# Low halves of eight weight tiles on GpSimd, one pair pooled by products with ones, and a new plan of the order

## The chip, the cores and the metric

The kernel runs on one core of a Trainium2 chip. Its engines are TensorE (PE: matmuls, with PEld for weight loads), VectorE (DVE), ScalarE (ACT), GpSimd (POOL) and SyncE (SP, which issues most DMAs). Each works through its own list of instructions in order and waits on semaphores for the others. The metric is the device time of one execution in microseconds.

## The reference

Inputs q, k, v have shape 4 x 8 x 576 x 64 (batches, heads, positions, width). Two attentions are added, and their sum goes through two MLPs:

```python
q_d = q.reshape(B, H, Sd, 4, D).mean(axis=3)          # k_d, v_d likewise
out_up = np.repeat(sm_attn(q_d, k_d, v_d), 4, axis=2) # pooled attention
scores = np.where(np.abs(pos[:, None] - pos[None, :]) < 4, scores, -1e9)
out_local = softmax(scores) @ v                       # banded attention
x = (out_up + out_local).transpose(0, 2, 1, 3).reshape(2304, 512)
h = x @ w_in;  x = (h / (1 + exp(-h))) @ w_out        # first MLP, 512-2048-512
h = x @ w2_in; r = max(h, 0); out = (s * r * r + b) @ w2_out
```

Inputs and outputs are float32 or carried with float32 accuracy: the kernel splits each operand into a high half and a low half and makes three products (high-high, low-high, high-low) of each.

## The kernel before

The whole program is recorded first and ordered afterwards. `W.op(engine, cost, fn, w, r, pr)` (line 106) records one piece of work with an assumed cost, what it writes and reads, and a priority `pr`. `plan` (line 139) then walks through time and gives each engine the candidate that can start soonest, by least `pr` among equals; an op with two engines (EITHER) goes to the one that would be done first. The result is a fixed order on each engine. The priorities are formulas of constants at the top of the file (`P_IN`, `DEC0`, `RATE` and so on). Where the plan has PE idle in the head, `run` fills the gap with `spin<-idle` matmuls (lines 387 to 394), 64 columns of bfloat16 zeros whose result nobody reads; the last of them reads `split[0]`, the finished split of the first block.

Work goes in these stages. In the head (about 0 to 48 us) batch 0 goes through both attentions, one pair of heads at a time (i = 0 to 3): q, k and v rows are loaded (`nat`), turned by PE, pooled by fours (`dq`, `dk`, L670), scored, and the banded part is done through `pB`, `be`, `pBT`, `bat`, `pBO`. The sum `xf` is split into `xh` and `xl` (L585, L586), one piece per pair: four pieces, and then the first MLP can run. Beside it the first MLP's weights are decoded: 16 tile pairs (`wi`, `wo`) come as pairs of 32-bit words (`wi_raw`, `wo_raw`) and become float32 in `to_f32` by ACT (L401) and two integer ops on DVE (L404 a shift, L411); `halves` then makes the high half by a cast (L415, ACT or DVE) and the low half by a subtraction (L417, DVE). Two `f32` buffers serve this decode.

From 48 us on the first MLP runs in five blocks of 512 tokens (the last 256): `hp` is the first product, `g` its silu on ACT (L951), `gh` and `gl` its halves (L952 ACT, L953 DVE), and `y` the second product. Between them batch 1's banded attention, and on DVE the local attention of batches 2 and 3, are done. From about 354 to 441 us the 32 tiles of the second MLP's weights are decoded to float32 by `whole` (L1085) and written to DRAM. The second MLP (from about 500 us) works on sums of them, `ha`, `hb`, `hc`, and then `oa`, `ob`, `oc`, `os`.

Loads of the head wait in the order of SP's queue; `NACT` says how many pairs' v rows go through ACT's queue instead (L979). Batch 1's loads wait for `split_end[D1 + D1S * hq]`, the end of the decode of one tile pair (L1005).

Of the kernel before, what the change touches and what calls it, by code (L numbers as in the profile page):

```python
# [38 lines left out]
TURN = 0.07  # L39
FLIGHT = 4  # L40
NW = 35
NACT, NACTV = 1, 0
NNAT, NVW = 10, 4
AHEAD = 4
MORE = 0.0
# [1 line left out]
NEARLY = 0  # L47
MASKED = False
ADDED = False
P_IN, P_OUT, P_Y0, P_W0, P_Y1, P_Y4, P_W, P_OS = 163.074, 237.937, 195.038, -36.246, 62.462, 102.369, 272.176, 169.42  # L50
P_STEP, P_BT, P_PO, P_PN = 6.074, -5.7, 16.567, 57.528
P_G, P_B, P_C = -45.097, 0.253, -5.619
D1, D1S = 8, 2
NWARM = 100
ACTW, ACTW2 = 0, True
TANH = 0
NOACC = 0
HEAD = 3
NLAST, LASTS = 3, [0, 1, 2]
VPE, QKPE = 0, 0  # L60
GPV, GPQ, GPS, GPM = 0, 0, 0, 0
PAIR = "AAAAAAAATTTTTTTTG0H101OOOO01OOOO01FFFFFFFF01I0101"
FILL0, FILLG, FILLD = 5.0, 0.12, 0.85
SLOW = 1.05
FAR = float(2 ** 33)


NAT0, NATS = -3.387, 1.422
VW0, VWS, VW1 = 6.355, 0.281, 27.579
RAWF, RAW0, RATE = 35.769, 5.781, 1.255  # L70
DECF, DEC0, DECS = 47.826, 49.984, 0.829
PT0, PTS = 31.757, 3.611
PN0, PNS = 5.815, 6.313
PB0, PBS = -2.568, 16.345
NAT1, PT1, PT1S = 33.957, 58.357, 3.543
LDP = 49.468


class Slot:
# [16 lines left out]
class Weave:  # L96
# [9 lines left out]
    def op(self, eng, cost, fn, w=(), r=(), pr=0.0, table=None):  # L106
        n, deps = len(self.ops), set()
        r = [x if isinstance(x, tuple) else (x, None) for x in r]
        w = [x if isinstance(x, tuple) else (x, None) for x in w]

        def hits(d, k):
            return [v for kk, v in d.items() if k is None or kk is None or kk == k]

        for b, k in r:
            deps.update(hits(b.wr, k))
        for b, k in w:
            deps.update(hits(b.wr, k))
            for v in hits(b.rd, k):
                deps.update(v)
        for b, k in r:  # L120
            b.rd.setdefault(k, []).append(n)
        for b, k in w:
            if k is None:
                b.wr, b.rd = {}, {}
            else:
                b.rd.pop(k, None)
            b.wr[k] = n
        deps.discard(n)
        bufs = []
        for b, _ in r + w:  # L130
            if b not in bufs:
                bufs.append(b)
                if not b.left and b.kind in self.turns:
                    self.turns[b.kind].append(b)
                b.left += 1
        self.ops.append((eng if isinstance(eng, tuple) else (eng,), cost, fn, sorted(deps), bufs, pr, table))
        return n
# [154 lines left out]
def kernel(ctx, tc, q, k, v, w1_in, w1_out, w2_in, w2_out, s2, b2, cst, out):  # L292
    nc = tc.nc
# [41 lines left out]
    op = W.op  # L335

    def mark(name):
        b = Buf(None, None, None, name)
        b.slot = Slot(None, None)
        return b  # L340
# [8 lines left out]
    def copy(eng, out, in_, by=1.0):  # L349
        if by == 1.0:  # L350
            (nc.scalar.copy if eng == "act" else nc.vector.tensor_copy)(out=out, in_=in_)  # L351
        elif eng == "act":
            nc.scalar.mul(out=out, in_=in_, mul=by)
        else:
            nc.vector.tensor_scalar(out=out, in0=in_, scalar1=by, scalar2=None, op0=ALU.mult)
# [42 lines left out]
    def to_f32(t, f, pr, end=(), more=0.0, by_act=True, early=False):  # L398
        top = lambda: t[:, :, :, 1]
        if by_act:  # L400
            op("act", 0.57 + more, lambda: nc.scalar.activation(  # L401
                out=f[:].bitcast(F32), in_=top().bitcast(F32), func=AF.Prelu, scale=2.0 ** -48, alpha=2.0 ** 32), w=[f], r=[t], pr=pr)
            by, engine = ("pool", nc.gpsimd) if early else ("dve", nc.vector)
            op(by, 0.75 if early else 0.335 + more, lambda: engine.tensor_scalar(  # L404
                out=f[:], in0=f[:], scalar1=3, scalar2=None, op0=ALU.logical_shift_left), w=[f], pr=pr)
        else:
            op("dve", 0.335 + more, lambda: nc.vector.tensor_scalar(
                out=f[:], in0=top(), scalar1=0x07FFFFFF, scalar2=3, op0=ALU.bitwise_and, op1=ALU.logical_shift_left), w=[f], r=[t], pr=pr)
            op("dve", 0.6 + more, lambda: nc.vector.scalar_tensor_tensor(
                out=f[:], in0=top(), scalar=-0x40000000, in1=f[:], op0=ALU.bitwise_and, op1=ALU.bitwise_or), w=[f], r=[t], pr=pr - 0.001)  # L410
        op("dve", 0.6 + more, lambda: nc.vector.scalar_tensor_tensor(  # L411
            out=f[:], in0=t[:, :, :, 0], scalar=29, in1=f[:], op0=ALU.logical_shift_right, op1=ALU.bitwise_or),
           w=[f, *end], r=[t], pr=pr - 0.001)

    def halves(f, o, pr, more=0.0, end=[]):  # L415
        op(EITHER, (0.52 + more, 0.34 + more), lambda eng: copy(eng, o[:, 0], f[:].bitcast(F32)), w=[(o, 0), *end], r=[f], pr=pr)
        op("dve", 0.6 + more, lambda: nc.vector.tensor_tensor(  # L417
            out=o[:, 1], in0=f[:].bitcast(F32), in1=o[:, 0].bitcast(F32), op=ALU.subtract), w=[(o, 1)], r=[f, (o, 0)], pr=pr - 0.001)

    def load_in(w_d, m, to):  # L420
        src = w_d[:, m * P:(m + 1) * P].bitcast(I32)
        dma(to.rearrange("p k f t -> p k (f t)"), src.rearrange("(k p) f -> p k f", p=P))

    def load_out(w_d, m, to):
        dma(to.rearrange("p k f t -> p (k f t)"), w_d[m * P:(m + 1) * P, :].bitcast(I32))

    def weights(m, pr, after, lpr=None):
        got = []
        end = mark("end")
        for nm in ("wi", "wo"):  # L430
            t = Buf("w", [P, KD, P, 2], I32, nm + "_raw")

            op("sp", (1, 1.45 if nm == "wi" else 1.27), lambda t=t, nm=nm: load_in(w1_in, m, t[:]) if nm == "wi" else load_out(w1_out, m, t[:]),
               w=[t], r=after, pr=pr if lpr is None else lpr)
            f = Buf("f32", [P, KD, P], I32, "f32")
            o = Buf("w", [P, 2, KD, P], F32R, nm)
            to_f32(t, f, pr, [end], 0.0, m >= ACTW, m < GPS)
            halves(f, o, pr)
            got.append(o)
        split_end[m] = end  # L440
        wts[m] = got
# [16 lines left out]
    def l_load(b, s0, ns, nm, pr):  # L458

        t = tens[nm]  # L460
        lo, wd = (0, ns) if nm == "q" else (HALO, ns + 2 * HALO)
        x = Buf("l" + nm, [P, 2, wd, D], F32, "l" + nm)

        def row(a):
            return (b * H + a) * S + s0 - lo

        def over(a):
            return b == B - 1 and a == 1 and s0 + ns == CH and nm != "q"

        def part(a, c0, n, q0, nq, w0, w1):  # L470
            p0 = c0 * KD + q0
            dma(x[p0:p0 + n * nq, a, w0:w1].rearrange("p w d -> p (w d)"),
                bass.AP(t.tensor, (row(a) + q0 * 2 * S + c0 * CH + w0) * D, [[CH * D, n], [2 * S * D, nq], [1, (w1 - w0) * D]]))

        def load():
            for a in range(2):
                if over(a):
                    part(a, 0, NCH, 0, KD, 0, wd - HALO)
                    part(a, 0, 28, 0, KD, wd - HALO, wd)
                    part(a, 28, 3, 0, KD, wd - HALO, wd)  # L480
                    part(a, NCH - 1, 1, 0, KD - 1, wd - HALO, wd)
                else:
                    part(a, 0, NCH, 0, KD, 0, wd)

        if over(1):
            op("dve", 0.3, lambda: nc.vector.memset(x[96:128, 1, wd - HALO:wd], 0.0), w=[x], pr=pr)
        op("sp", (5 if over(1) else 2, 0.26 * wd), load, w=[x], pr=pr)
        return x
# [8 lines left out]
    def local(b, s0, ns, pr):  # L497
        qs, ks, vs = l_load(b, s0, ns, "q", pr), l_load(b, s0, ns, "k", pr), l_load(b, s0, ns, "v", pr + LDP)
        sc = Buf("sc", [P, 2, ns, WIN], F32, "sc")
# [481 lines left out]
    for m in range(KF):  # L981
        weights(0, DECF, [], RAWF) if m == 0 else weights(m, DEC0 + DECS * m, [split_end[m - AHEAD]] if m >= AHEAD else [], RAW0 + RATE * m)
# [253 lines left out]
    def named(nm, names, at, pr):  # L1236
        for q in range(HF):
            o = Buf("u2", [P, 2, KD, P], F32R, "w" + nm)
            in_place(nm, q + at, o, 0, None, DM, 0.88, pr + 0.1 * q)
            for i, name in enumerate(names):  # L1240
                piece_of(name, q, o, i)
            yield
# [103 lines left out]
    def put(o, r0, e=None):  # L1346
# [11 lines left out]
        for by, mine in (("sp", parts_),) if e != 1 else (("sp", parts_[::2]), ("act", parts_[1::2])):  # L1358
# [6 lines left out]
            "F": named("t43", ("t4", "t3"), 0, P_B + 3 * P_C), "0": lead[0], "1": lead[1]}  # L1365
    for x in PAIR:
        if x in "GHI":
# [57 lines left out]
```

## Time and profile before

| | |
|---|---|
| median of 3 runs | 862.49 us (861.5 to 863.54) |
| profiled execution, own time | 861.29 us |
| its span | 859.4 us |
| PE busy | 850.0 us (99%) |
| DVE busy | 734.1 us (85%) |
| ACT busy | 507.7 us (59%) |
| POOL busy | 0.2 us |
| granted TensorE clock | 1.00 in every stretch |

The span is what the profiler recorded of one execution; the execution's own time is 1.9 us longer. "Busy" sums the time in which an engine had an instruction at work; neighbours on one engine overlap slightly, so the step from start to start is a little under the duration. The spin matmuls count as busy PE.

### The profile page before, as it was taken

How to read it: one execution, taken by the hardware profiler on the slowest of the kernel's cores; microseconds unless marked ns; L12 is line 12 of the kernel's file. 1: busy time of each engine (PE TensorE's matmuls, PEld its weight loads, DVE VectorE, ACT ScalarE, POOL GpSimd, SP SyncE). 2: the span in 40 equal slices, each digit the busy share in tenths (PEclk: the TensorE clock that was granted, in tenths of full speed). 3: DMA queues.
4: the chain of work that ended last, by engine and by line, in shares of the span. 5: the costliest groups of instructions: out<-in, count | busy, mean ns of one | idle time of the engine just before them, and what ended most of it. 6: DMA issues, size and time to landing. Idle time of an engine off the chain costs nothing.

```text
span 859.4 us, 14697 instructions
## 1 busy us (share of the span) xinstructions
PE 850.0 (99%) x5300; PEld 714.5 (83%) x5300; DVE 734.1 (85%) x1364; ACT 507.7 (59%) x1034; POOL 0.2 (0%) x4
## 2 busy tenths in 40 slices
PE   9999999999999999999999999999999999999998
PEld 8878777778778878888889988888888988888887
DVE  7999996999999999987667788777787999888894
ACT  6998797656456742454456566666666665444351
POOL 0000000000000000000000000000000000000000
PEclk9999999999999999999999999999999999999999
DMA  8995421642444221388985246666679866443311
GB/s 217 319 351 151 132 68 41 191 130 70 106 127 112 77 69 39 123 278 304 330 297 176 86 119 212 205 189 183 184 248 286 274 183 213 160 143 125 123 33 42
DMA packets 157426, 144.26 MB, mean 168 GB/s; under 512 B 65452, under 2 KB 125738, under 8 KB 157354
## 3 DMA queue, kind: packets, MB, share of 16 engines
q1 hardware_dynamic: 156946, 142.96, 53.2%
q8 instruction: 42, 0.69, 0.3%
q10 hardware_dynamic: 408, 0.36, 0.1%
q14 instruction: 30, 0.25, 0.1%
HBM read 102.40 MB, written 40.89 MB: 167 GB/s over the span
## 4 chain that ended last, share of the span: by engine, by line
PE 87%; DVE 7%; ACT 2%; DMA 2%; issue 1%; SPq 0%; ACTq 0%; DVEq 0%
PE hp L926 23%; PE y L926 20%; PE ha L926 10%; PE oa L1286 6%; PE hc L926 5%; PE oc L1286 4%; PE ob L1286 4%; PE oa L1293 3%; PE hb L926 2%; PE oc L1293 2%; PE ob L1293 2%; PE pS L703 1%; DMA wo_raw<-in_moe_w_out_dram 1%; PE pB L842 1%; PE pU L742 1%
## 5 line engine op out<-in xcount | busy, mean ns | idle before, releaser
L926 PE MATMUL hp<-xh,wi 128*128 128x512 f32 (+1 forms) x640 | 200.8, 377 | 0.3 <-ACT g L951 0.3
L926 PE MATMUL y<-gh,wo 128*128 128x512 f32 (+1 forms) x640 | 199.8, 375 | 0.0
L926 PEld LDWEIGHTS hp<-xh,wi 128*128 128x128 f32 x640 | 116.9, 188 | 23.3 <-ACT g L951 2.8
L926 PEld LDWEIGHTS y<-gh,wo 128*128 128x128 f32 x640 | 117.0, 189 | 19.9 <-issue 0.8
L926 PE MATMUL y<-gl,wo 128*128 128x512 f32 (+1 forms) x320 | 118.2, 369 | 0.0
L926 PE MATMUL hp<-xl,wi 128*128 128x512 f32 (+1 forms) x320 | 118.0, 369 | 0.0
L926 PE MATMUL ha<-yh,wi 128*128 128x512 f32 x256 | 86.4, 390 | 0.8 <-ACT g L351 0.8
L952 ACT CAST gh<-g 128x512 fp32r<-128x512 f32 (+1 forms) x80 | 46.2, 577 | 54.2 <-PE y L926 53.3
L951 ACT ACTIVATE g<-hp 128x512 f32<-128x512 f32 (+1 forms) x80 | 44.4, 555 | 41.4 <-DVE gl L953 36.3
L926 PEld LDWEIGHTS y<-gl,wo 128*128 128x128 f32 x320 | 60.4, 189 | 8.7 <-DVE gl L953 0.2
L926 PEld LDWEIGHTS hp<-xl,wi 128*128 128x128 f32 x320 | 60.4, 189 | 8.1
L1139 ACT ACTIVATE g<-g,sbt 128x512 f32<-128x512 f32 (+1 forms) x70 | 53.4, 769 | 23.2 <-DVE g L1134 22.8
L953 DVE TENSOR_TENSOR gl<-g,gh 128x512 fp32r<-128x512 f32 (+1 forms) x80 | 50.5, 631 | 14.5 <-ACT gh L952 14.4
L1134 DVE SCALAR_TENSOR_TENSOR g<-g 128x512 f32<-128x512 f32 (+1 forms) x80 | 49.8, 633 | 9.8 <-ACT g L1133 9.1
L926 PEld LDWEIGHTS ha<-yh,wi 128*128 128x128 f32 x256 | 48.1, 188 | 10.9 <-ACT g L351 1.3
L1267 ACT CAST gh<-gs 128x1024 fp32r<-128x1024 f32 x27 | 28.4, 1052 | 46.7 <-DVE gs L1263 38.7
L1267 ACT CAST gh<-graw 128x1024 fp32r<-128x1024 f32 x36 | 37.6, 1051 | 27.7 <-PE ob L1293 11.6
L926 PE MATMUL ha<-yl,wi 128*128 128x512 f32 x128 | 50.0, 390 | 0.0
L1268 DVE TENSOR_TENSOR gl<-graw,gh 128x1024 fp32r<-128x1024 f32 x36 | 43.6, 1217 | 6.8 <-PE oa L1286 4.1
L351 ACT COPY g<-ha 128x512 f32<-128x512 f32 x48 | 28.1, 585 | 28.0 <-PE ha L926 23.8
L926 PE MATMUL hc<-yh,wi 128*128 128x512 f32 x128 | 44.6, 389 | 0.0
L543 DVE TENSOR_TENSOR tmp<-le,lv 128x1344 f32<-128x1344 f32 (+1 forms) x28 | 37.9, 1353 | 0.5
(197 smaller groups left out, 1721.1 us busy)
## 6 DMA issues: line engine op xcount, KB each, us to landing
graw<-gd SPq DMA_DIRECT2D x36, 512.0 KB
gd<-g SPq DMA_DIRECT2D x64, 256.0 KB
wi_raw<-in_moe_w_in_dram SPq DMA_DIRECT2D x16, 512.0 KB
wo_raw<-in_moe_w_out_dram SPq DMA_DIRECT2D x16, 512.0 KB
w_raw<-in_moe_w_in_dram SPq DMA_DIRECT2D x16, 512.0 KB
w_raw<-in_moe_w_out_dram SPq DMA_DIRECT2D x16, 512.0 KB
nq<-in_q_dram SPq DMA_DIRECT2D x32, 144.0 KB
nk<-in_k_dram SPq DMA_DIRECT2D x32, 144.0 KB
```

Of the source, the lines that this page charges most:

```text
L351: (nc.scalar.copy if eng == "act" else nc.vector.tensor_copy)(out=out, in_=in_)
L543: op("dve", dve(n * WIN * D), lambda t=t, i0=i0, n=n, h2=h2: nc.vector.tensor_tensor(out=t[:], in0=wide(e[:, h2 * ns + i0:h2 * ns + i0 + n ...
L926: nc.tensor.matmul(t(), lhsT=lhs(i), rhs=rhs(i), start=(first and i == 0), stop=(last and i == 2), **kw)
L951: op("act", act(n), lambda g=g, hp=hp: nc.scalar.activation(out=g[:], in_=hp[:], func=AF.Silu), w=[g], r=[hp], pr=-5, table="silu")
L952: op("act", act(n), lambda g=g, gh=gh: nc.scalar.copy(out=gh[:], in_=g[:]), w=[gh], r=[g], pr=-5)
L953: op("dve", dve(n), lambda g=g, gh=gh, gl=gl: nc.vector.tensor_tensor(out=gl[:], in0=g[:], in1=gh[:].bitcast(F32), op=ALU.subtract), w=[gl ...
L1134: op("dve", dve(n) + 1.5 * MORE, lambda: nc.vector.scalar_tensor_tensor(out=t[:], in0=t[:], scalar=0.0, in1=t[:], op0=ALU.max, op1=ALU.mul ...
L1139: nc.scalar.activation(out=t[:], in_=t[:], func=AF.Identity, scale=sbt[:, 0:1], bias=sbt[:, 1:2])
L1267: op("act", act(HF * P) + MORE, lambda: nc.scalar.copy(out=flat(hi), in_=flat(x)), w=[hi], r=[x], pr=pr + n)
L1268: op("dve", dve(HF * P) + MORE, lambda: nc.vector.tensor_tensor(out=flat(lo), in0=flat(x), in1=flat(hi).bitcast(F32), op=ALU.subtract), w= ...
L1286: nc.tensor.matmul(bank[:].rearrange("p x n -> p (x n)"), lhsT=hi[:, q], rhs=w(), start=new and q == 0, stop=False, skip_group_check=True)
L1293: nc.tensor.matmul(bank[:, 0], lhsT=lo[:, q], rhs=w()[:, 0], start=False, stop=q == HF - 1, skip_group_check=True)
```

## The change

Five constants that are not priorities change: `NACT` 1 to 0 (the v rows of the first pair go to SP's queue), `D1S` 2 to 0 (all of batch 1's loads wait for tile pair 8 alone), `ACTW2` True to False (the second weights are decoded without ACT), `QKPE` 0 to 1 (the last pair's q and k of batch 0 are pooled by PE), and the new `GPH` = 4 (low halves of the tile pairs m < 4 go to GpSimd). All priorities are new numbers, so the order changes on every engine. From line 419 on the line numbers of after are 2 higher.

```diff
-NACT, NACTV = 1, 0
+NACT, NACTV = 0, 0
-P_IN, P_OUT, P_Y0, P_W0, P_Y1, P_Y4, P_W, P_OS = 163.074, 237.937, 195.038, -36.246, 62.462, 102.369, 272.176, 169.42
+P_IN, P_OUT, P_Y0, P_W0, P_Y1, P_Y4, P_W, P_OS = 55.274, 296.499, 156.769, 163.771, 85.099, 150.133, 277.946, 173.606
...
-D1, D1S = 8, 2
+D1, D1S = 8, 0
-ACTW, ACTW2 = 0, True
+ACTW, ACTW2 = 0, False
-VPE, QKPE = 0, 0
+VPE, QKPE = 0, 1
+GPH = 4
...
-    def halves(f, o, pr, more=0.0, end=[]):
+    def halves(f, o, pr, more=0.0, end=[], early=False):
         op(EITHER, (0.52 + more, 0.34 + more), lambda eng: copy(eng, o[:, 0], f[:].bitcast(F32)), w=[(o, 0), *end], r=[f], pr=pr)
-        op("dve", 0.6 + more, lambda: nc.vector.tensor_tensor(
+        by, engine = ("pool", nc.gpsimd) if early else ("dve", nc.vector)
+        op(by, 1.35 if early else 0.6 + more, lambda: engine.tensor_tensor(
             out=o[:, 1], in0=f[:].bitcast(F32), in1=o[:, 0].bitcast(F32), op=ALU.subtract), w=[(o, 1)], r=[f, (o, 0)], pr=pr - 0.001)
...
-            halves(f, o, pr)
+            halves(f, o, pr, early=m < GPH)
```

With `QKPE` = 1 the function `down` takes its first branch for the last pair of batch 0: 12 matmuls of the `nat` tiles with `fours` (a matrix of ones in groups of four) give the sums in PSUM (`pd`), from which `q_diag` and `dk` are copied. With `ACTW2` False, `to_f32` takes its second branch for the second weights: a mask and shift that reads every second word of `w_raw`, a two-operand op that also reads `w_raw`, and L411 as before.

On DVE, around the fourth `xl` piece (the last L586 of the head), before has this. `f_1104` and the like are the f32 buffers of the weight decode, `wo` and `wi` the tiles:

```order
L404 TENSOR_SCALAR f_1104<-f_1104 128x512
L404 TENSOR_SCALAR f_1110<-f_1110 128x512
L411 SCALAR_TENSOR_TENSOR f_1104<-wi_raw,f_1104 128x512
L411 SCALAR_TENSOR_TENSOR f_1110<-wo_raw,f_1110 128x512
L417 TENSOR_TENSOR wi<-f_1104,wi 128x512
L905 TENSOR_TENSOR xf<-pBO,upT 128x256 x2
L417 TENSOR_TENSOR wo<-f_1110,wo 128x512
L404 TENSOR_SCALAR f_1165<-f_1165 128x512
L586 TENSOR_TENSOR xl<-xf,xh 128x512
L411 SCALAR_TENSOR_TENSOR f_1165<-wo_raw,f_1165 128x512
```

And after has this at the same place:

```order
L412 SCALAR_TENSOR_TENSOR f_1077<-wi_raw,f_1077 128x512
L352 CAST wi<-f_1077 128x512
L907 TENSOR_TENSOR xf<-pBO,upT 128x256
L405 TENSOR_SCALAR f_1129<-f_1129 128x512
L907 TENSOR_TENSOR xf<-pBO,upT 128x256
L412 SCALAR_TENSOR_TENSOR f_1129<-wo_raw,f_1129 128x512
L405 TENSOR_SCALAR f_1137<-f_1137 128x512
L412 SCALAR_TENSOR_TENSOR f_1137<-wi_raw,f_1137 128x512
L588 TENSOR_TENSOR xl<-xf,xh 128x512
```

The low halves are gone from DVE ahead of `xl`, and the integer ops of later tiles stand there in their place. The low halves are on POOL, which had no such rows; after has eight, in this order:

```order
L419 TENSOR_TENSOR wi<-f_772,wi 128x512
L419 TENSOR_TENSOR wo<-f_844,wo 128x512
L419 TENSOR_TENSOR wi<-f_906,wi 128x512
L419 TENSOR_TENSOR wo<-f_1040,wo 128x512
L419 TENSOR_TENSOR wi<-f_1077,wi 128x512
L419 TENSOR_TENSOR wo<-f_1129,wo 128x512
L419 TENSOR_TENSOR wi<-f_1137,wi 128x512
L419 TENSOR_TENSOR wo<-f_1191,wo 128x512
```

The integer ops of the first seven of these tiles end, on DVE, ahead of the fourth `xl`; none of these rows stood on POOL before.

On PE, behind the first blocks' second products (`y`), before goes from the turned band weights `pBT` straight to the product `pBO`:

```order
L926 MATMUL y_1278<-gh,wo 128x512
L926 MATMUL y_1278<-gl,wo 128x512
L926 MATMUL y_1278<-gh,wo 128x512
L883 MATMUL pBT<-csb,be 72x128 x4
L896 MATMUL pBO<-bat,vw 64x64 x8
L926 MATMUL y_1258<-gh,wo 128x512
```

After has first products (`hp`) between them:

```order
L928 MATMUL y_1256<-gh,wo 128x512
L885 MATMUL pBT<-csb,be 72x128 x4
L928 MATMUL hp<-xh,wi 128x512
L928 MATMUL hp<-xl,wi 128x512
L928 MATMUL hp<-xh,wi 128x512 x2
L928 MATMUL hp<-xl,wi 128x512
L928 MATMUL hp<-xh,wi 128x512
L898 MATMUL pBO<-bat,vw 64x64 x8
```

Six `hp` matmuls moved in between `pBT` and the `pBO` that needs its copy `bat`.

## Rows read from the trace of the kernel before

**Rows 1.** Busy us by stretch; columns: stretch, length, engines, clock, DMA share, GB/s.
```profile
6.00:48.00 42.00, 41.06 (x711) 35.34 (x709) 40.53 (x118) 37.66 (x142) 0.00 (x0) 1.00 0.98 298
48.00:340.00 292.00, 290.31 (x1722) 229.68 (x1722) 277.63 (x544) 189.10 (x431) 0.00 (x0) 1.00 0.39 113
340.00:450.00 110.00, 110.00 (x491) 90.78 (x490) 85.99 (x165) 56.15 (x94) 0.00 (x0) 1.00 0.76 263
450.00:500.00 50.00, 50.00 (x396) 48.81 (x394) 37.69 (x71) 30.31 (x68) 0.00 (x0) 1.00 0.36 119
```

**Rows 2.** What PE waited for; total us, times, longest.
```profile
PE oa L1286 <- DVE os L1301: 1.3, 1, 1.3
...
PE ha L926 <- ACT g L351: 0.8, 1, 0.8
PE pBO L896 <- ACT gh L952: 0.8, 1, 0.8
```

**Rows 3.** Groups on PE, 0 to 60 us; columns: busy, mean ns, idle before.
```profile
L389 PE MATMUL spin<-idle 128*128 128x64 bf16 x368 | 15.3, 204 | 1.0 <-DVE idle L385 1.0
...
L775 PE MATMUL pq<-csb,nq 96*128 96x96 f32 x24 | 2.9, 251 | 0.0
```

**Rows 4.** Timeline of PE at the last spin; columns: start, duration.
```profile
47.53 0.39 PE L926 MATMUL hp<-xl,wi 128*128 128x512 f32 x1
...
47.99 0.20 PE L389 MATMUL spin<-idle 128*128 128x64 bf16 x1
```

**Rows 5.** Timeline of DVE, 42 to 58 us.
```profile
46.49 0.42 DVE L404 TENSOR_SCALAR f<-f 128x512 int32<-128x512 int32 x1
46.83 0.68 DVE L586 TENSOR_TENSOR xl<-xf,xh 128x512 fp32r<-128x512 f32 x1
47.43 0.68 DVE L411 SCALAR_TENSOR_TENSOR f<-wo_raw,f 128x512 int32<-128x512 int32 x1
...
57.25 0.69 DVE L351 COPY bat<-pBT 72x512 f32<-72x512 f32 x1 [0.79 <-PE pBT L883]
```

**Rows 6.** Timeline of DVE, 0 to 10 us.
```profile
3.44 0.25 DVE L597 TENSOR_REDUCE fours<-csb 96x24 f32<-96x96 f32 x1 [1.91 <-DMA csb<-in_const_dram]
4.76 0.69 DVE L632 TENSOR_TENSOR nv<-nv 72x512 f32<-72x512 f32 x1 [1.07 <-DMA nv<-in_v_dram]
...
7.04 0.75 DVE L670 TENSOR_REDUCE dq<-qkT 128x144 f32<-128x576 f32 x1 [1.13 <-ACT qkT L353]
```

**Rows 7.** Groups on DVE, 0 to 75 us; columns: busy, mean ns, idle before.
```profile
L417 DVE TENSOR_TENSOR wi<-f,wi 128x512 fp32r<-128x512 f32 x9 | 6.2, 685 | 0.2
...
L860 DVE TENSOR_TENSOR be<-be,bst 128x288 f32<-128x288 f32 x9 | 4.0, 449 | 0.1
...
L361 DVE TENSOR_SCALAR de<-de,dst 96x144 f32<-96x144 f32 x9 | 2.1, 284 | 0.0
...
L355 DVE TENSOR_SCALAR q_diag<-dq 64x144 f32<-64x144 f32 x3 | 0.9, 298 | 0.1
...
L351 DVE COPY dat<-pT 72x288 f32<-72x288 f32 x2 | 0.8, 444 | 0.0
```

**Rows 8.** Timeline of the queues of ACT and SP at the start.
```profile
0.72 1.00 ACTq L364 DMA_DIRECT2D nv<-in_v_dram  x2
...
0.73 0.42 SPq L364 DMA_DIRECT2D csb<-in_const_dram  x1
...
3.31 0.91 SPq L364 DMA_DIRECT2D band<-in_const_dram  x1
```

**Rows 9.** Two wider DVE lines; ns min/median/max.
```profile
L543 DVE TENSOR_TENSOR tmp<-le,lv x28: 1082/1545/1560, 199.6 to 418.5; 128x1344 f32<-128x1344 f32 x16, 128x896 f32<-128x896 f32 x12
...
L1268 DVE TENSOR_TENSOR gl<-graw,gh x36: 1210/1216/1226, 660.8 to 838.5; 128x1024 fp32r<-128x1024 f32 x36
```

**Rows 10.** Timeline of PE at the pBO gap.
```profile
56.60 0.60 PE L883 MATMUL pBT<-csb,be 128*72 128x128 f32 x4
58.04 0.69 PE L896 MATMUL pBO<-bat,vw 72*64 72x64 f32 x16 [0.83 <-ACT gh L952]
```

More of the change, by code (lines that the diff above doesn't have):

```diff
@@ L49 @@
 ADDED = False
-P_IN, P_OUT, P_Y0, P_W0, P_Y1, P_Y4, P_W, P_OS = 163.074, 237.937, 195.038, -36.246, 62.462, 102.369, 272.176, 169.42
-P_STEP, P_BT, P_PO, P_PN = 6.074, -5.7, 16.567, 57.528
-P_G, P_B, P_C = -45.097, 0.253, -5.619
-D1, D1S = 8, 2
+P_IN, P_OUT, P_Y0, P_W0, P_Y1, P_Y4, P_W, P_OS = 55.274, 296.499, 156.769, 163.771, 85.099, 150.133, 277.946, 173.606
+P_STEP, P_BT, P_PO, P_PN = 15.448, 17.279, 19.494, 87.644
+P_G, P_B, P_C = 122.069, -51.265, -0.653
+D1, D1S = 8, 0
 NWARM = 100
-ACTW, ACTW2 = 0, True
+ACTW, ACTW2 = 0, False
 TANH = 0
@@ L65 @@
 FAR = float(2 ** 33)
[L68 to L76, printed above, removed]
+NAT0, NATS = -5.076, 2.193
+VW0, VWS, VW1 = 4.429, 0.221, 44.145
+RAWF, RAW0, RATE = 23.241, 9.451, 2.906
+DECF, DEC0, DECS = 50.831, 48.143, 1.077
+PT0, PTS = 18.996, 6.055
+PN0, PNS = 11.151, 6.473
+PB0, PBS = 2.956, 13.985
+NAT1, PT1, PT1S = 38.862, 57.698, 5.555
+LDP = 45.556
 class Slot:
```

## The prediction

> **What bounds the kernel now.** I read first the table of busy time by stretch [rows 1]: TensorE (PE) is busy 41.06 of 42.00 us in 6:48, 290.31 of 292.00 in 48:340, 110.00 of 110.00 in 340:450 and 50.00 of 50.00 in 450:500. The list of what PE waited for comes second [rows 2]: behind the start only 1.3, 0.8 and 0.8 us at the largest places. So from 48 us on the kernel is bound by PE, and an edit that only takes work off another engine there buys nothing. Before 48 us the picture is false: 368 of PE's matmuls are "spin" matmuls on a zero tile, which the planner writes into gaps that it foresees, the last of them at 48.0 us [rows 3]. The head is not full of work; it waits for data, and dense work starts only when the fourth and last `xl` piece of the first block is there. PE's timeline shows it [rows 4]: the matmul of that piece starts at 47.53, 0.02 after VectorE's (DVE) `xl` ends (46.83 + 0.68 = 47.51, [rows 5]), and the last spin follows at 47.99. DVE works without a gap from 7.04 us [rows 6] to 56.5, where it waits 0.79 us for pBT [rows 5]. So the total is nearly: the moment at which DVE reaches the fourth `xl`, plus a dense stretch whose matmuls stay the same in number, plus what PE still waits in it. The change can move the first, and add to or take from the last.
>
> **The change part by part.** Steps of DVE are taken from starts of neighbours, which overlap a little: 46.49 to 46.83 for a one-input shift (0.34), 46.83 to 47.43 for a two-input 128x512 (0.60) [rows 5]; other means are in [rows 7], each taken less the same overlap of about 0.08; casts go at the shift's step, the copy of upT at that of q_diag.
>
> *Head, DVE.* Up to the fourth `xl`, the order of before and after differs by: five low halves (L417) fewer, 5 x 0.60 = -3.01; two pooling reduces fewer (0.75 each, [rows 6], less overlap), 2 x 0.66 = -1.33; one band product (L860) fewer, -0.37; three scaled copies of pq replaced by two plain ones, -0.37; and, pulled forward by the new plan, two more L411 +1.20, one shift +0.34, two casts +0.68, three `de` scalings +0.61, and one copy each of bat, dat, upT and q_diag, +0.61 +0.37 +0.22 +0.22. Sum -5.08 + 4.25 = -0.83 us. The planner spent most of what it saved on work which it moved ahead of the mark. I take -0.8; bounds -3.0 (nothing pulled forward counted) and 0.
>
> *Head, the v rows.* The first pair's `nv` loads leave ACT's queue, where they were issued at 0.72 us, for SP's, behind csb, nq and nk, so at about 3.31, where band was issued before [rows 8]. Csb, issued at 0.73, was waited for until 3.44, 2.7 us later [rows 6, 8]; by that nv lands near 6.1, and its two sums (0.69 for the first, [rows 6], less for the shorter second) stand ahead of dq on DVE, which can then start near 7.2 to 7.4 instead of 7.04. I take +0.3; bounds 0 and +1.07, the wait for nv that shows now.
>
> *Head, PE.* Twelve small matmuls on `fours` replace the two reduces. The nearest rows are 24 transposes of nq of 251 ns each [rows 3]; with overlap 12 cost at most 3.0, as a row of pipelined ones about 1.3. They stand where the plan has 37 spins fewer, so they fall into waiting time; if that cover were gone, +1.3 at most on this path. I take 0.
>
> *Eight low halves on GpSimd (POOL).* POOL does nothing in before [rows 1], so no row has the price. Bounds: 0.68, DVE's own L417 [rows 7], and 1.55, DVE's row of 128x1344 [rows 9]; I take 1.22, the row of 128x1024, as if the two operands were read one after the other [rows 9]. Those who wait are PE's third product of a tile, and ACT's conversion of the tile after next, which reuses the f buffer. Each tile is decoded well before its use while spins fill PE; at 1.22 I cost the wait at 0, bounds 0 and +0.9 (one op late once, 1.55 - 0.68). The Trainium skill, "GPSIMD Engine Reference", section 3.1, puts a two-input elementwise op at 2.6 cycles an element, about twice VectorE's time; as an estimate that is near 1.3 us, which changes nothing above; no run shows it yet. What POOL does to DVE meanwhile is priced between 0 and a full 1.22 per op, and this is the main unknown (rival B). I take 0, since no row shows one engine's SBUF access stretching the other's.
>
> *Start of the dense stretch.* -0.8 + 0.3 = -0.5.
>
> *The gap at 57 us.* Before, PE ran pBT at 56.60, and pBO waited 0.83 us and started at 58.04 [rows 10], behind DVE's copy of bat (57.25, [rows 5]). After, five rows of `hp` matmuls stand between pBT and pBO, 6 x 0.23 = 1.4 us of work (0.23 is the step of [rows 4]: 47.53 to 47.99 for two). That covers the wait: -0.8; bounds -1.0 and 0 (if the `hp` group itself waits for its weights).
>
> *The second weights, 340 to 450 us.* 32 tiles lose ACT's conversion (ACT is off the path) and the shift on `f`, and get a shift from `w_raw` at every second element and one more two-input op: 32 x 0.60 = 19.3 us more on DVE [rows 5]. The new order also puts two products and two reduces of the local attention into this stretch (about 4 x 1.0) and takes out about 2.6 of short pieces. DVE's idle time there is 110.0 - 86.0 = 24.0 us [rows 1] against 20.6 more. It just fits; I take +0.3; bounds 0 and +7.5 (rival C).
>
> *The rest.* PE's order is the same from 480 us on, so the waits for `os` (1.3) and `ha` (0.8) [rows 2] stay. Batch 1's loads now all wait on the decode of one tile pair (number 8) instead of 8, 10, 12 and 14, so they are never later: 0.
>
> Sum: -0.5 - 0.8 + 0.3 = -1.0 on the profiled execution's own 861.29 (span 859.4 and 1.9 around it), 860.3. The median shown is 862.49, 1.2 higher, so the forecast is 861.5.
>
> **The rivals.** A is the sum above.
>
> B: POOL shuts DVE out. If DVE stood still whenever both engines read SBUF with two operands, each POOL op would cost DVE part of its 1.22 us. By the order five to seven can run ahead of the fourth `xl`; I count five. From all of it, 5 x 1.22 = 6.1, subtract the DVE rows that read PSUM or one operand; laying POOL's rows beside DVE's in the new order leaves 2.2 (only two-input neighbours stopped) to 4.1 (copies and shifts too), say 3. It decides from 0.16 us per op, where the gain of 0.8 is eaten. Then 861.5 + 3 = 864.5. For it: the removed low halves and the added ones are of the kind that reads two full SBUF operands. Against it: the trace has no POOL work at all. [...]
>
> C: slower by the second weights. The shift from `w_raw` reads every second element. The contiguous shift takes a 0.34 step, against 0.60 for a two-input op; if stride takes away its pace, 32 x 0.26 = 8.5 us more, 20.6 + 8.5 = 29.1 against 24.0 idle, and `gl` comes late while PE waits. It decides once the extra passes 24 us. Its price is the overflow of 5.1, up to 7.5 with uneven pieces, less what block order hides: +4, so 865.5. For it: PE has no spare time there. Against it: 450:500 has 12.3 us of DVE idle [rows 1], and DVE often waits for ACT's gh, which ACT, 32 conversions lighter, delivers sooner.
>
> D: the larger gain. With the low halves gone from DVE, the first `gl` come 2.4 to 7.9 us earlier in DVE's order, counted in steps, and PE's small waits up to 340 us (292.0 - 290.31 = 1.7 [rows 1]) go too: of these 0.8 is counted, so -0.9 more, and without the SP term and the +0.3: 861.5 - 1.5 = 860.0. Against it: most of the 1.7 are changes of matmul shape, whose number stays.
>
> E: the change does not do what it says, because the DVE time it frees is spent again ahead of the mark: 862.3.
>
> **How the numbers follow.** A 0.45, B 0.27, C 0.12, D 0.11, E 0.05. Within 0.2% is within 1.7 us of 862.49, about what a measurement of this kernel tells from no change. A at 861.5 gives faster 0.3, same 0.65; B slower 0.75; C slower 0.95; D faster 0.8, same 0.2. Faster 0.45 x 0.3 + 0.11 x 0.8 + a little of B = 0.24, taken as 0.27 since bounds reach further down than up on the head's DVE term; slower 0.27 x 0.75 + 0.12 x 0.95 + 0.02 = 0.34; same 0.39. The range goes from 859.2, D with the whole of its waits gone, to 865.8, C. A alone spans 860.0 to 863.0.
>
> **What would show it.** Right: eight POOL rows near 1.2 us; the fourth `xl` near 46.3 and the last spin near 47.5; no 0.8 gap before pBO; DVE near 106 of 110 in 340:450 with PE still full; waits for os and ha unchanged. Wrong by B: DVE rows beside POOL's rows with starts more than 0.60 apart, and the last spin at 49 or later. Wrong by C: a strided shift of about 0.68 busy (0.60 step), and PE waits for `gl` in 340:450. A first dq at 8 us or later would make the v rows the culprit.

## The result, and the profile after

The changed kernel takes 867.81 us (median of 5 runs, 867.16 to 870.34) against 862.49 for the kernel before (861.5 to 864.5 in the runs beside it): ratio 1.0062, 95% interval 1.0045 to 1.0079. It is slower by 5.3 us, where 861.5 was forecast; 867.81 lies above the stated range. The profiled execution took 867.16 (span 865.4), 5.9 more than that of before.

The tile view of the spin matmuls, after (columns: ns min/median/max, first and last start), says in which stage the time went:

```profile
L390 PE MATMUL spin<-idle x331: 190/193/258, 1.0 to 53.9; 128*128 128x64 bf16 x166
```

The last spin starts at 53.9 and no longer at 47.99 [rows 4]: 5.9 us later. Ahead of it TensorE (PE) has the same products in both kernels, 27 `hp` rows among them, and after has 24 rows of pooling products (`pd`) more. The span grew by 6.0. So the head lost all of it, and what the dense stretch won and lost cancels. The last spin is a place in PE's list and not a sign that the fourth `xl` is there: its matmul reads only the zero tile, and its tie to `split[0]` binds the plan alone. After, it ran while the fourth `xl` was still at work (53.15 to 54.92, below).

Why the head is late is read first from VectorE (DVE) and GpSimd (POOL). Here is the start of DVE's timeline, after:

```profile
2.68 0.25 DVE L599 TENSOR_REDUCE fours<-csb 96x24 f32<-96x96 f32 x1 [1.13 <-DMA csb<-in_const_dram]
7.53 0.69 DVE L634 TENSOR_TENSOR nv<-nv 72x512 f32<-72x512 f32 x1 [4.60 <-DMA nv<-in_v_dram]
8.13 0.74 DVE L672 TENSOR_REDUCE dq<-qkT 128x144 f32<-128x576 f32 x1
```

DVE waits 4.60 us for nv, where before it waited 1.07, and its first dq starts at 8.13 where it was 7.04 [rows 6]. Then the timelines of POOL and of DVE side by side, after (a row may join neighbours, "x3"):

```profile
33.12 1.27 POOL L419 TENSOR_TENSOR wi<-f,wi 128x512 fp32r<-128x512 f32 x1 [32.68 <-DVE wi L352]
39.19 1.31 POOL L419 TENSOR_TENSOR wo<-f,wo 128x512 fp32r<-128x512 f32 x1 [4.80 <-DVE wo L352]
41.66 1.27 POOL L419 TENSOR_TENSOR wi<-f,wi 128x512 fp32r<-128x512 f32 x1 [1.16 <-DVE dst L718]
47.32 1.46 POOL L419 TENSOR_TENSOR wo<-f,wo 128x512 fp32r<-128x512 f32 x1 [4.39 <-ACT wo L352]
...
52.90 1.48 POOL L419 TENSOR_TENSOR wo<-f,wo 128x512 fp32r<-128x512 f32 x1 [2.47 <-ACT wo L352]
54.34 1.75 POOL L419 TENSOR_TENSOR wi<-f,wi 128x512 fp32r<-128x512 f32 x1
```

```profile
33.29 1.13 DVE L718 TENSOR_SCALAR dst<-dst 96x3 f32<-96x3 f32 x1
...
39.56 0.43 DVE L870 TENSOR_REDUCE bst<-be 128x4 f32<-128x288 f32 x1
39.91 0.61 DVE L874 TENSOR_SCALAR bst<-bst 128x4 f32<-128x4 f32 x1
...
41.89 0.16 DVE L720 RECIPROCAL dst<-dst 96x3 f32<-96x3 f32 x1
41.98 1.27 DVE L862 TENSOR_TENSOR be<-be,bst 128x288 f32<-128x288 f32 x1
...
47.69 1.38 DVE L352 CAST wi<-f 128x512 fp32r<-128x512 f32 x1
50.48 0.42 DVE L907 TENSOR_TENSOR xf<-pBO,upT 128x256 f32<-128x256 f32 x1 [1.41 <-PE pBO L898]
...
52.54 0.69 DVE L412 SCALAR_TENSOR_TENSOR f<-wi_raw,f 128x512 int32<-128x512 int32 x1
53.15 1.77 DVE L588 TENSOR_TENSOR xl<-xf,xh 128x512 fp32r<-128x512 f32 x1
54.85 0.45 DVE L849 TENSOR_TENSOR be<-pB,band 128x288 f32<-128x288 f32 x1
```

Lay the ends beside each other. POOL's first row ends at 34.39; the scalar op on 96x3 numbers that started at 33.29 ends at 34.42. POOL's second ends at 40.50, the next scalar op at 40.52. The third ends at 42.93, and `be`, which takes 0.45 elsewhere [rows 7], ends at 43.25, 0.32 behind it. The fourth xl starts at 53.15, and ends 0.54 behind POOL's end of 54.38. In each of these DVE gets on only when POOL is through. It also goes the other way: POOL's row at 52.90 takes 1.48 instead of 1.27; DVE's two-operand row of 52.54 was at work when it began. Not every DVE row is stopped. The reduce at 39.56 runs under POOL's row in its usual 0.43, the reciprocal at 41.89 in 0.16, and the `be` row at 54.85, one of whose two operands lies in PSUM, in 0.45.

The third effect is in the table by stretch, after (columns as in [rows 1]; the last three are PE's granted clock, the DMA share and GB/s):

```profile
40.00:44.00 4.00, 2.37 (x60) 2.20 (x60) 4.00 (x12) 2.76 (x15) 1.77 (x2) 1.00 1.06 365
44.00:48.00 4.00, 4.00 (x26) 3.15 (x24) 3.93 (x11) 2.65 (x5) 0.68 (x1) 0.57 1.07 403
```

and in PE's timeline, after:

```profile
43.39 0.60 PE L885 MATMUL pBT<-csb,be 128*72 128x128 f32 x4 [1.63 <-DVE be L862]
...
46.12 1.05 PE L928 MATMUL hp<-xh,wi 128*128 128x512 f32 x2
...
48.80 0.48 PE L928 MATMUL hp<-xh,wi 128*128 128x512 f32 x1
```

PE waits 1.63 us for `be`, is busy 2.37 of 4 us, and then its clock reads 0.57 over the next 4 us (1.2 instead of 2.4 GHz for most of it): two `hp` matmuls take 1.05 there and 0.62 at 51.33. This is one execution; a second profile of after, and a kernel without POOL's low halves, have nearly the same wait and no fall behind it (below).

What PE waited for (the waits view, after):

```profile
PE pBT L885 <- DVE be L862: 2.3, 2, 1.6
...
PE hp L928 <- ACT g L953: 0.8, 2, 0.6
PE pt L560 <- DVE rc L536: 0.6, 1, 0.6
PE ha L928 <- ACT g L352: 0.5, 1, 0.5
```

The waits of pBO (0.8) and of `os` (1.3) [rows 2] are gone; 1.4 us of new ones stand in 340 to 450 us. The table by stretch there, after:

```profile
340.00:450.00 110.00, 108.64 (x482) 88.72 (x481) 101.42 (x189) 33.40 (x53) 0.00 (x0) 1.00 0.76 255
```

PE lost 1.36 us there [rows 1: 110.00 before].

### The profile page after: what moved, and what is told of

The parts are those of the page before. It is cut to its first block, busy times and chain, and to the rows that moved or that the text cites. A ratio compares the mean times of both kernels' runs of the same rounds, so it can differ in the third digit from the quotient of the medians.

```text
span 865.4 us, 14619 instructions
## 1 busy us (share of the span) xinstructions
PE 855.6 (99%) x5287; PEld 718.6 (83%) x5287; DVE 755.4 (87%) x1397; ACT 490.3 (57%) x994; POOL 11.3 (1%) x12
## 5 line engine op out<-in xcount | busy, mean ns | idle before, releaser
L928 PE MATMUL hp<-xh,wi 128*128 128x512 f32 (+1 forms) x640 | 203.0, 380 | 0.9 <-ACT g L953 0.8
L928 PE MATMUL y<-gh,wo 128*128 128x512 f32 (+1 forms) x640 | 197.6, 374 | 0.0
L928 PEld LDWEIGHTS ha<-yh,wi 128*128 128x128 f32 x256 | 48.1, 188 | 11.4 <-ACT g L352 1.7
```

The costliest lines, as they stand in the source:

```text
L928: nc.tensor.matmul(t(), lhsT=lhs(i), rhs=rhs(i), start=(first and i == 0), stop=(last and i == 2), **kw)
```

## The experiments

Kernels named a_ start from after, those named b_ from before. Ratios are to the kernel before, run on the same chip beside it. "Order kept" means that only the engine or queue of some instructions differs.

**GpSimd off, or on, alone.** Two kernels move only the engine of the eight low halves:

```diff
 a_low_dve (order kept)
-        by, engine = ("pool", nc.gpsimd) if early else ("dve", nc.vector)
+        by, engine = ("pool", nc.vector) if early else ("dve", nc.vector)
 b_low_pool (order kept; m < 4)
-        op("dve", 0.6 + more, lambda: nc.vector.tensor_tensor(
+        op("dve", 0.6 + more, lambda: nc.gpsimd.tensor_tensor(
```

> After, with its order kept, but the eight low halves run on VectorE at the place where the plan has them on GpSimd. Theory L (GpSimd and VectorE shut each other out of SBUF): in after five VectorE rows beside GpSimd's rows are stretched by 0.97, 0.45, 0.82, 0.96 and 1.09, 4.3 us ahead of or at the fourth xl; here no row is stretched, six low halves of 0.60 come back (3.6), and what followed from the stretches (PE's wait of 1.63 before a pBT at 43.4, half clock at 44 to 48) goes: last spin 50.5 to 52 instead of 53.9, time 864.3 to 866. Rival V (the late v rows cause the whole shift, GpSimd is innocent): last spin 54 or later, since VectorE has 3.6 us more, 868 to 871.

> Before, with its order kept, but the eight low halves of the first four tile pairs run on GpSimd at the places where they stood on VectorE. Theory L (shared access shuts one engine out): GpSimd rows of about 1.3 us, VectorE rows beside them stretched by up to 1.1 us, so that the 5 x 0.60 saved ahead of the fourth xl are given back, and the products that need a low half wait for GpSimd; time 862.0 to 865. Rival A (no mutual effect): the fourth xl comes 3.0 us earlier, time 859 to 860.5.

b_low_pool: 864.29, ratio 1.0026 (1.0015 to 1.0038), with the clock at 0.999 or 1.00 in all ten executions. So the clock is not in it, and the eight low halves on GpSimd cost the kernel before about 2.2 us; the predicted relief of 3.0 did not come. DVE's timeline of b_low_pool shows the same stop beside POOL's first row (31.16 to 32.43):

```profile
31.00 1.72 DVE L361 TENSOR_SCALAR de<-de,dst 96x144 f32<-96x144 f32 x3
```

Three such rows take 0.69 in after where POOL is idle (at 43.16). The stop is not the whole cost: in the same trace PE waits 0.51 us for a low half from POOL (at 53.46), and DVE twice 1.0 us for ACT's `f`, waits that before does not have. The last spin comes 1.0 us later (49.03), and the rest of what this profiled execution lost (866.21, one of the two slowest) lies behind the head.

a_low_dve: 866.32, ratio 1.0068 (1.0046 to 1.0091). In its trace no DVE row is stretched: the scalar op at 34.07 takes 0.16 again,

```profile
34.07 0.16 DVE L718 TENSOR_SCALAR dst<-dst 96x3 f32<-96x3 f32 x1
```

but the median fell only within the noise, and the wait that theory L put down to the stretch stayed. PE's timeline, a_low_dve:

```profile
43.10 0.60 PE L885 MATMUL pBT<-csb,be 128*72 128x128 f32 x4 [1.53 <-DVE be L862]
```

Without a stretched row `be` is as late, since a low half now stands ahead of it on DVE. Behind this wait the clock stays at 1.00 (44 to 48 us). The last spin comes at 52.1. Its four executions were 863.94 at clock 1.00, and 865.28, 867.36 and 869.04 at 0.996 to 0.997: the spread goes with the clock and is not GpSimd's.

**The v rows, alone and with the low halves.**

```diff
 a_vact (order kept), and a_vact_low (with a_low_dve's edit)
-                queue = nc.scalar if by == "act" else nc.sync
+                queue = nc.scalar if by == "act" or (b, i, nm) == (0, 0, "v") else nc.sync
```

> After, with the v rows of the first pair issued from ACT's queue as in before; nothing else. Rival V: nv is used at 4.8 instead of 7.53, the first dq at 7.0 instead of 8.13, every later piece moves by 1.1 to 2.8 and the time falls by as much, 865.0 to 866.7. Theory L: the first xl moves from 25.7 to about 24.5, but the stretched rows stay, so the last spin stays at 52 or later and the time at 866.3 to 867.8.

> After, with both edits: v rows of the first pair from ACT's queue and the eight low halves on VectorE. If L and V each hold a part, the parts add: last spin 49 to 51, time 863 to 864.8. If one alone is the cause, this equals the better of the two single edits within 0.8.

a_vact: 868.14, ratio 1.0079 (1.0062 to 1.0095). nv is used at 4.92, dq starts at 7.00, the first xl at 24.8 instead of 25.7, and the last spin at 53.05 instead of 53.9: the head won 0.9 us in the profiled execution. The median shows no gain, with the clock down in all four, and both theories missed the time. The late v rows alone are not the cause. a_vact_low: 864.16, ratio 1.0042 (1.0025 to 1.0059), its interval below that of a_vact: with nv early, taking GpSimd away wins some 4 us (868.14 to 864.16), the clock included (a_vact's executions are all at 0.996 to 0.998). The time lies where the parts were to add, the last spin (52.8 in the profiled execution, at a fallen clock) not. Its executions again part by clock: 863.22, 863.61 and 863.99 at 1.00; 864.34, 866.7 and 867.45 at 0.997 to 0.998.

**The clock.** a_spin puts 48 spins into PE's wait of 1.63 us (`fill(48)` ahead of the seventh pBT).

> After, with 48 more spin matmuls (48 x 0.033 = 1.6 us) on PE just ahead of the seventh pBT group, where PE waits 1.63 us at 41.7 to 43.4 before its clock reads 0.52 and 0.63 at 44 to 48. Theory C (that wait halves the clock, and the slow matmuls cost 1.5 to 2 us of the shift): the clock stays at 1.00, last spin 52 to 52.5, time 866 to 866.5. Theory L: the clock stays at 1.00, but the next product waits for GpSimd's low half (48.6) and VectorE's stretched rows anyway: last spin 53.3 to 53.9, time 867.2 to 867.8.

870.17, ratio 1.0095 (1.0076 to 1.0115): a miss for both theories. In its profile the clock holds at 44 to 48, but reads 0.50 at 24 to 30, a place where the profile of after had 1.00. That after itself falls there too in some executions shows in its second profile (a_again, below). The place is behind the pooling products of the change. PE's timeline, after:

```profile
20.73 0.72 PE L744 MATMUL pU<-dat,nv 72*64 72x144 f32 x8
21.38 1.52 PE L655 MATMUL pd<-fours,nq 96*128 96x24 f32 x12
22.83 1.15 PE L898 MATMUL pBO<-bat,vw 72*64 72x64 f32 x32
23.91 1.52 PE L655 MATMUL pd<-fours,nk 96*128 96x24 f32 x12
25.27 0.45 PE L777 MATMUL pq<-csb,nk 96*128 96x96 f32 x3
```

No spin stands here; before had 18 at 20.19 and 32 at 21.90. Whether that alone moves the clock was tried on before: b_nospin leaves those two groups out, where PE would only wait.

```diff
 b_nospin
-                    self.fill(int((begin[i] - now) * FILLD / 0.03))
+                    n = int((begin[i] - now) * FILLD / 0.03)
+                    if n not in (18, 32):
+                        self.fill(n)
```

> Before, with two groups of spin matmuls left out (18 at 20.2 us and 32 at 21.9 us, on both sides of a pBO); PE then just waits there, and no real work changes. Theory Q (with few columns through PE between 20 and 25 us its clock falls, whatever the pooling does): the granted clock reads about 0.5 for some us from 23 to 25 on, last spin later by 1 to 4 us, time 862.5 to 866. Rival P (the fall in b_qkpe belongs to the pd products or to chance): clock 1.00, time as before within 0.5.

865.19, ratio 1.0034 (1.002 to 1.0049), and all ten executions have a mean clock of 0.992 to 0.998. The table by stretch, b_nospin:

```profile
20.00:24.00 4.00, 2.04 (x43) 1.79 (x42) 4.00 (x15) 4.00 (x23) 0.00 (x0) 0.87 0.91 214
24.00:28.00 4.00, 4.00 (x35) 3.64 (x34) 2.80 (x10) 2.79 (x8) 0.00 (x0) 0.50 1.07 297
28.00:32.00 4.00, 4.00 (x60) 3.23 (x60) 2.57 (x6) 3.05 (x11) 0.00 (x0) 0.77 1.03 343
```

PE is busy half of 20:24, and the next 4 us run at 0.50. DVE is busy only 2.80 of 4 us there, since it waits for PE's products (2.20 us for pS, up to 29.00). Fifty matmuls whose result nobody reads are worth about 3 us.

**The pooling products.** b_qkpe gives before only `QKPE` = 1; b_qkpe_pad, a_pad and a_vact_low_pad add `fill(3)` behind each of the twelve products (to b_qkpe, after and a_vact_low); a_low_pad is a_pad with a_low_dve's edit; a_qkpe0 gives after `QKPE` = 0. b_qkpe and a_qkpe0 are planned anew, so their order differs everywhere.

> Before, with only the pooling of the last pair by products with ones, planned by before's own constants. Theory Q (these 24-column matmuls, and the spins they displace, let PE's clock fall in the head): the granted clock reads 0.5 for some us behind the pd rows in most executions, mean clock 0.995 to 0.998, time 862.5 to 865.5 and a wider spread of runs. Rival: the products are hidden and VectorE has 1.33 us less: clock 1.00, 860.0 to 861.3.

> b_qkpe (874.31) with three spin matmuls behind each of the twelve pooling products (36 x 0.033 = 1.2 us on PE). Theory Q: the clock stays at 1.00 in 20 to 32 us, and of the 12 us that b_qkpe lost 5 to 9 come back: 865 to 869.5. Rival R (b_qkpe is slow by the order that was planned anew, not by the clock): 872 to 876.

> After, with the last pair pooled on VectorE again (two reduces, 1.33 us), planned anew by after's constants. Theory Q: the clock stays at 1.00 up to 40 us in every execution; with it the slow executions go, time 864.5 to 866.5. Theory L alone: VectorE has 1.33 us more ahead of the fourth xl, GpSimd's stretches stay, 867.5 to 869.

b_qkpe: 874.31 (1.0103 to 1.0171), with clocks of 0.993 to 0.996; 0.50 is read at 22 to 28, right behind its pooling products. b_qkpe_pad: 872.44 (1.0099 to 1.0133), three of four at 0.998: the clock was better and most of the loss stayed, as the rival expected. The fourth, which was profiled (875.27), reads 0.50 at 24 to 32 us in spite of the padding. a_qkpe0: 873.6 (1.0096 to 1.0163): the clock holds up to 40 us, and the kernel is still slower than after, so theory Q's time was missed. One option under constants drawn for the other costs 6 to 12 us, by the order that was planned anew and the clock together; these three say little about the products themselves.

> After, with three spin matmuls behind each of the twelve pooling products; nothing else. Theory Q: the falls at 24 to 31 us go; the fall at 44 to 48 behind VectorE's stretched row stays, so 865.5 to 867 with a spread under 2. Rival: no change, 867 to 870, since all executions of after lose their clock at 44 us alone.

> After, with three parts undone or mended at once: first v rows from ACT's queue, low halves on VectorE, spins between the pooling products. If lock, late v rows and clock are the whole loss, no execution shows a clock below 0.999 and the time is 862.5 to 863.8, within 0.3% of before. If the new order itself costs time in the head (three integer ops and more pulled ahead of the fourth xl), the last spin stays at 51 or later and the time at 863.8 to 865.

> a_pad (867.67, its clock at 1.00 in three of four executions) with the eight low halves on VectorE. The pair prices GpSimd alone, without the clock. Theory L: 864.3 to 866.3, 1.5 to 3.5 us under a_pad, no stretched row. Rival (the new order and the late v rows are the whole loss): 867 to 869, since VectorE has 3.6 us more ahead of the fourth xl.

> After itself once more, on the chip of the two runs beside it, so that they have it as a yardstick: 867 to 869, with the clock below 0.999 in most executions.

a_pad: 867.67 (1.0049 to 1.0087); three of four executions at clock 1.00, and those took 866.82 to 868.01. So with the padding the clock held more often, and after is not faster by it. (The fourth, which was profiled, 869.71, still reads 0.59 at 44 to 48 us.) a_low_pad: 867.06 (1.0048 to 1.0076), four of six at 1.00, no stretched row; its distance to a_pad is within the noise. That is a miss for theory L, which wanted 864.3 to 866.3, and lies where the rival put it (867 to 869). a_vact_low_pad: 866.49 (1.003 to 1.0066); expected were at most 865. a_again, after once more: 869.53 (1.0068 to 1.0092), all five at 0.994 to 0.998, a little above the 869 expected; its table by stretch shows the early fall:

```profile
24.00:28.00 4.00, 4.00 (x28) 3.75 (x26) 2.58 (x10) 1.45 (x6) 0.00 (x0) 0.56 0.82 222
28.00:32.00 4.00, 4.00 (x53) 3.46 (x54) 1.95 (x7) 2.88 (x11) 0.00 (x0) 0.59 1.02 378
```

In this execution PE waits 1.63 us for `be` from 44.87 on, and the clock behind it stays at 1.00.

With no GpSimd, early v rows and spins between the products, a_vact_low_pad stays 0.3 to 0.7% above before. What is left is after's order with the pooling products in it (2.7 us on PE), and the new spins' own 1.2 us.

**The second weights.** b_w2dve: before with `ACTW2` False; the order differs from 354 us on.

> Before, with only the second weights decoded without ACT; the order differs from about 354 us on. Theory W (VectorE has too little idle time there): VectorE is busy over 101 of 110 us in 340:450, PE waits 1 to 2.5 us for g, gl or rc, time 862.1 to 863.6. Rival: PE stays full there, 860.6 to 861.6.

862.31, ratio 1.0005 (0.999 to 1.0021): no cost that can be measured. DVE is busy 100.96 of 110 us, PE 109.81. The strided shift goes at the contiguous one's pace, as the groups of after in 340:450 show (busy, mean ns):

```profile
L408 DVE TENSOR_SCALAR f<-w_raw 128x512 int32<-128x512 int32 x31 | 13.0, 424 | 3.7 <-DMA w_raw<-in_moe_w_out_dram 1.5 <-DMA w_raw<-in_moe_w_in_dram 1.4 <-DMA w2out<-f 0.9
```

**The gap at 57 us.** b_gap gives before the one thing that after's order did better:

```diff
 b_gap (two hp groups ahead of pBO)
+        order.insert(331, order.pop(338))
+        order.insert(332, order.pop(342))
```

> Before, with two hp groups (6 matmuls, 1.4 us) moved ahead of the pBO that waits 0.83 us at 57.2 to 58.0: the one place where the order of after did better. Theory G (the gap is lost time on the bounding engine): the wait goes and the dense stretch ends 0.6 to 0.9 earlier, 0.1% under before, within what the runs can tell. Rival: the wait moves to the y group behind it, which needs gl (57.97 to 58.66), no gain.

864.62, ratio 1.0025 (1.0014 to 1.0036): slower, a miss for both. PE's timeline, b_gap:

```profile
57.12 0.60 PE L885 MATMUL pBT<-csb,be 128*72 128x128 f32 x4
59.92 0.50 PE L928 MATMUL hp<-xh,wi 128*128 128x512 f32 x1 [2.19 <-ACT g L953]
60.26 0.40 PE L928 MATMUL hp<-xl,wi 128*128 128x512 f32 x1
60.49 0.88 PE L928 MATMUL hp<-xh,wi 128*128 128x512 f32 x2
```

The `hp` group waits 2.19 us for ACT's `g`, which has to empty its PSUM bank first, and its last row shown is slow again (0.88 for two). A wait of 0.8 was traded for one of 2.2.

No variant tried beats before. Not tried alone were `D1S` and the priorities.

## Why the prediction was wrong, point by point

Two steps failed: what ends the head (with the pooling products put at nothing), and what POOL does to DVE.

*What ends the head: a step that failed.* The prediction let dense work start when DVE delivers the fourth xl, and read this from the `hp` row at 47.53, 0.02 after that xl ended. By the kernel's order the nine groups of `hp` products ahead of the last spin belong to the first three pieces, in both kernels. The row at 47.53 is of a third piece, and the closeness was chance. The fourth xl is first read behind the last spin. PE's timeline, before:

```profile
49.10 0.39 PE L926 MATMUL hp<-xl,wi 128*128 128x512 f32 x1
```

and after:

```profile
53.62 0.49 PE L390 MATMUL spin<-idle 128*128 128x64 bf16 x11
...
55.02 0.45 PE L928 MATMUL hp<-xl,wi 128*128 128x512 f32 x1
```

Before, this is 1.6 us after the xl ended (47.51); after, 0.1 us (54.92). What filled PE before was its own list: from 40.64 up to the last spin it has neither a spin nor a wait worth naming. The spins stand in that list in a fixed number, and PE runs them whether or not it would have to wait. So the head has a sum on PE too, up to the row behind the last spin (rows from start to start, waits as gaps):

| PE, us | row behind the last spin | spins | waits | pooling products | other products |
|---|---|---|---|---|---|
| before | 48.1 | 13.7 (368) | 1.9 | 0 | 32.5 |
| after | 54.0 | 13.2 (331) | 3.5 | 2.8 | 34.5 |
| a_low_dve | 52.3 | 13.2 (331) | 3.3 | 2.8 | 32.9 |
| a_vact_low_pad | 52.0 | 13.7 (367) | 2.7 | 2.7 | 32.8 |

Of after's 5.9 us the pooling products are the largest single term, 2.8. The prediction took 0 for them: "they fall into waiting time". But of waiting PE had only 1.9 us before, 1.0 of it at the very start, and the 37 spins fewer gave back 0.5. The waits add 1.6, and the other products 2.0, of which 1.6 is missing in a_low_dve, the same order at clock 1.00. The price was too low as well: the prediction counted twelve rows, but each of the twelve calls is two rows in the trace (x12 twice). This is a sum of rows and no experiment: with the products taken out and the order kept, which was not run, PE might wait in their place, as in b_nospin.

The sum for DVE is the moment at which it starts the fourth xl, split into its idle time, what POOL's rows stretched it by, and the rest, its work. (Idle is summed from the gaps in DVE's timeline, stretch from rows over 0.25 us longer than the median of the same operation and form.)

| fourth xl, us | start | idle | stretched | work |
|---|---|---|---|---|
| before | 46.83 | 5.41 | 0 | 41.4 |
| after | 53.15 | 9.14 | 3.20 | 40.8 |
| a_low_dve | 52.21 | 7.92 | 0 | 44.3 |
| a_vact_low_pad | 51.94 | 7.50 | 0 | 44.4 |
| predicted | 46.3 | 5.7 | 0 | 40.6 |

*GpSimd: the other step that failed.* The prediction set what POOL does to DVE at 0, "since no row shows one engine's SBUF access stretching the other's", and held the opposite as rival B at 0.27. B's mechanism runs: 3.20 us ahead of the fourth xl and 1.09 within it, against the 3 priced. It ate the 3.0 that the prediction had DVE win, and on the order of before the move alone costs time (b_low_pool). It is not the whole 5.3 us: with the low halves back on DVE after stays 0.5 to 0.9% above before (a_low_dve). The POOL rows themselves, 1.27 to 1.31 where nothing stops them, are near the 1.22 taken. The Trainium skill, "SBUF — State Buffer", section "Who interferes with whom", says that the engine that issues second waits until the first is done, that copies, casts and scalar ops can be stopped as well as ops with two SBUF inputs, and that reduces never are. The rows above agree in each point, the unhindered reduce (0.43) included. An absence of rows was taken for evidence of no effect, though the kernel before had no POOL work that could have shown one.

*B's time was too low,* since it counted only DVE's lost time on top of A. In the profiled execution PE's clock fell to 0.57 at 44 to 48 us, and DVE waited 1.41 for a late pBO (the row at 50.48), part of the 3.73 us of new idle time in DVE's table; a_low_dve, at clock 1.00, has no such wait there. That the stretch of `be` brought the fall about is not shown: the wait ahead of it is 1.53 us without any stretch.

*The v rows: mis-sized.* +0.3 was taken with 1.07 as the upper bound. nv came into use at 7.53, not at 6.1, behind csb and four loads of q and k rows on the same queue; dq moved by 1.1, and DVE's idle time up to the first xl grew from 5.17 to 7.15, 2.0 us. The estimate carried the delay of a lone transfer (csb's 2.7) over to one that stood behind four others. The prediction's sign for the v rows as the culprit (a first dq at 8 us or later) came true, and yet a_vact, which undoes them, moves the last spin by 0.9 us and the median not at all.

*DVE's work: nearly right.* -0.8 was forecast, -0.6 came. With the low halves back on DVE it is 2.9 more than before: after's order pulls the decode of later tiles ahead of the fourth xl, which the order showed and the prediction counted, but only against low halves that were supposed to cost DVE nothing.

*The pooling products' side effect: missed.* The plan put them where 50 spins had stood. b_nospin shows that spins are no free cover: without 50 of them the clock halves and the kernel loses 0.34%. How much of after's 5.3 us is this is not settled: a_pad runs mostly at clock 1.00 and is no faster, while within a_low_dve and a_vact_low the executions with a fallen clock are up to 5 us longer.

*The gap at 57 us* went as forecast, and so did *the second weights* (rival C falls: b_w2dve is equal to before; 101 of 110 us busy, 106 forecast). In after PE still waits 1.4 us there, which b_w2dve does not show (0.2), so it goes with after's order in that place (a_low_dve, with the same order, waits 0.5). The wait for `os` was to stay and went, although the order there is the same; why was not tried.

Shown, then: some rows of GpSimd and VectorE stop each other (rows of two kernels), and the low halves on GpSimd, alone on before, cost 0.26% instead of winning; missing spins halve PE's clock (+0.34% alone); `ACTW2` has no cost that can be measured alone; the v rows alone are not the cause. Inferred by what is left over: the new order with its pooling products, without GpSimd and late v rows, costs about 2 to 3 us (a_vact_low at clock 1.00: 863.2 to 864.0, against a median of 861.1 for before beside it), and PE's sum puts most of this down to the products (2.7 of the 3.9 us by which a_vact_low_pad's head is longer). Open: how the 5.3 us divide, since each repair exposed the next wait, and the parts do not add.

## What to carry to other kernels

Work moved to an idle engine is not free if that engine shares a path with the busy one: write the moved rows beside those of the busy engine, and count for the neighbour that meets one up to its whole length. Before calling a matmul the last piece's, count the pieces in the order. Dummy matmuls in a fixed number are work in PE's list and no slack; add up that list before putting new work at nothing. They can hold the clock too: before displacing them, count what is left in the place, and look at the granted clock of several executions, since one profile may show none of the falls or only one. And where an order is planned by drawn constants, one option flipped under them (b_qkpe, a_qkpe0) can cost more by order than the option is worth, so undo a part with the order kept.

## What the runs showed of the hardware that was not expected

A scalar op on 96x3 numbers (0.16 us) is held for the whole rest of a GpSimd row (1.13). A GpSimd row is held likewise: 1.75 us for one that began at 54.34, while the fourth xl ran to 54.92. A shift that reads every second 32-bit word takes 0.424 us, as the contiguous one does (0.422). The clock fell in different places of the same kernel: at 44 to 48 us in one execution of after and at 24 to 31 us in another, where the same wait of 1.63 us had no fall behind it.
